# Output products of the last token block in one pass, kv beside x, and four banks for h, in a tuned attention-and-MLP kernel

## The chip, the cores and the metric

The kernel runs on one core of one Trainium2 chip. The metric is device time in microseconds (us), the median over several executions. An execution is marked slow where it is clearly longer than others of its kernel or shows a lower granted TensorE clock; all runs of this study were of the fast state, at a granted clock of 0.998 to 1.00. Verdicts are "faster", "same" or "slower" at 2%, with a 95% interval. Engines are named as in the profile: PE is TensorE, PEld its weight loads, DVE VectorE, ACT ScalarE, POOL GpSimd, SP SyncE.

## The reference, cut to what matters

```python
def _attn_ref(q, k, v):            # (8 batches, 8 heads, 576 tokens, 64)
    q_s = softmax(q, axis=-1)      # over the head's 64 elements
    k_s = softmax(k, axis=2)       # over the tokens
    kv = np.einsum('bhsd,bhse->bhde', k_s, v)
    return np.einsum('bhsd,bhde->bhse', q_s, kv)

def _moe_ref(x, w_in, w_out, beta):     # x: 4608 x 512, d_ff = 2048
    h = x @ w_in
    g = h * (1.0 / (1.0 + np.exp(-beta * h)))
    return g @ w_out
```

(The softmax lines are shortened here: the reference subtracts the maximum and divides by the sum.) So each batch needs a small product kv, a product x of q with kv, and then two large products, h and the output, which is accumulated in "acc".

## The kernel before

Tokens go through in nine chunks of 512: batches 0 to 6, then the 64 last tokens of every batch as one chunk, then batch 7. A chunk has 16 slices j of the hidden layer. For each j, PE makes h (four matmuls of 128x128 weights and 512 columns), ACT makes tanh of it, DVE makes g from tanh and h, and PE adds g's product with w_out to four acc banks, one for each block of 128 tokens ("block 0" to "block 3"). PSUM, the memory that the matmuls write, is used here as eight banks: four for acc, two called "h" and two called "att", each pair used in turn. In the code below, comments are added and cuts marked:

```python
    HB, AB = ["b1", "b2"], ["b0", "b3"]
    turns = {"h": 0, "att": 0}

    def bank(tag):
        if tag not in turns:
            return tag
        turns[tag] += 1
        return (HB if tag == "h" else AB)[(turns[tag] - 1) % 2]

    def kv_mm(b):                       # 40 matmuls in tiles of 128x64, 65 columns
        t = att_of[b] = ps.tile([P, HP, D1], F32, tag=bank("att"), bufs=1, name=f"kv{b}")
        # ... cut: loops over heads and token blocks, tile_position=(0, r * D)

    def kv_norm(b):                     # two DVE instructions that read kv's bank
        # ... cut

    def x_quad(c):                      # 8 matmuls in tiles of 64x64, 512 columns
        xr = [ps.tile([P, MAIN], F32, tag=bank(("att", "h")[kt // 2]), bufs=1, name=f"x{c}_{kt}") for kt in range(KT)]
        # ... cut: matmuls with tile_position=(r * D, a * D), then four casts to SBUF

    def mm_b(c, j, sts=None):           # acc += g * w_out, one matmul for each token block
        # ... cut

    SEQ = {
        # ... cut
        2: 'h0 p15 h1 h2a h3a b0 h4 b1 h5 b2 h6a h7 b3 h8 b4 h9 b5 h10 b6 h11 b7 h12 b8 h13 b9 h14 b10 h15 b11 b12 x0 b13 b14',
        # ... cut
    }
```

In SEQ, h is the four matmuls of one slice (with "a" in an att bank), b the four output matmuls of one slice, p the last b of the chunk before, x the product with kv for the next chunk. Kv of the next chunk is made after h9. Between the h of a chunk the other engines also get the q and k exponentials, sums and products of coming chunks ("side" work).

The softmax here doesn't subtract the row's maximum and nothing guards it: scores larger than these inputs give would overflow.

Of the kernel before, what the change touches and what calls it, by code (L numbers as in the profile page):

```python
# [9 lines left out]
BF16 = mybir.dt.bfloat16  # L10
F32 = mybir.dt.float32
# [6 lines left out]
def kernel(  # L18
# [10 lines left out]
    nc = tc.nc  # L29
# [18 lines left out]
    if LASTMAIN:  # L48
        order[B - 1], order[B] = B, B - 1
    LASTC = order[-1]  # L50

    const = ctx.enter_context(tc.tile_pool(name="const", bufs=1))
    stage = ctx.enter_context(tc.tile_pool(name="stage", bufs=1))
# [131 lines left out]
    def k_exp(b, s, n=2):  # L185
        if s == 0:
            ek_buf(b)
        m = H // n
        h = slice(s * m, (s + 1) * m)
        nc.scalar.activation(  # L190
            ek[b][:, :, h, :].rearrange("p i h d -> p h i d"),
            k_st[b][:, h, 0 : R * D].rearrange("p h (i d) -> p h i d", i=R),
            ACTF.Exp,
        )
# [9 lines left out]
    def v_buf(b):  # L204
        t = work.tile([P, HP * RW * D1], BF16, tag="va", bufs=2, name=f"va{b}")
        if b < NW:
            va[b] = t[:].rearrange("p (j i x) -> p j i x", j=HP, i=RW)
        else:
            va[b] = t[:, 0 : R * H * D1].rearrange("p (i h x) -> p i h x", i=R, h=H)
        nc.gpsimd.memset(va[b][:, :, :, D:D1], 2.0)  # L210
# [9 lines left out]
    def v_cast(b, eng):  # L220
        evac(
            eng,
            va[b][:, :, :, 0:D].rearrange("p i h d -> p h i d"),
            v_st[b][:, :, 0 : R * D].rearrange("p h (i d) -> p h i d", i=R),
        )

    def vtail_cast(b, eng):
        e = b % 2
        rr = slice(e * TAIL, (e + 1) * TAIL)
        eng.tensor_copy(vt[(b // 2) % 2][rr, e, :, 0:D], v_st[b][rr, :, R * D : R * D + D])  # L230
# [51 lines left out]
# [5 lines that stand above are left out]
# [43 lines left out]
                kvp[r, b, j : j + n, e * D : (e + 1) * D], t[r, :, 0:D], rk[r].to_broadcast((D, n, D)), ALU.mult  # L330
            )

    def kv_mm(b):
        t = att_of[b] = ps.tile([P, HP, D1], F32, tag=bank("att"), bufs=1, name=f"kv{b}")
        for j in range(HP):
            for i in range(R + 1):
                for r in range(2):
                    hd = j // 2 * 4 + 2 * r + j % 2
                    nc.tensor.matmul(  # L339
                        t[r * D : (r + 1) * D, j, :],  # L340
                        ek[b][:, i, hd, :] if i < R else ekt[(b // 2) % 2][:, ds(hd * D, D)],
                        va[b][:, i, hd, :] if i < R else vt[(b // 2) % 2][:, b % 2, hd, :],
                        start=(i == 0),
                        stop=(i == R),
                        tile_position=(0, r * D),
                    )

    def kv_norm(b):
        t = att_of.pop(b)
        rk = work.tile([P, HP, 1], F32, tag="rk", bufs=2, name=f"rk{b}")  # L350
        nc.vector.reciprocal(rk[:], t[:, :, D:D1])
        nc.vector.tensor_tensor(kvq[:, b - NW], t[:, :, 0:D], rk[:].to_broadcast((P, HP, D)), ALU.mult)

    def x_quad(c):
        xr = [ps.tile([P, MAIN], F32, tag=bank(("att", "h")[kt // 2]), bufs=1, name=f"x{c}_{kt}") for kt in range(KT)]
        for b in range(B) if c == B else (c,):
            i, e = divmod(b, 2)
            cols = ds(b * TAIL, TAIL) if c == B else slice(0, MAIN)
            if b < NW:
                for j in range(HP):  # L360
                    nc.tensor.matmul(  # L361
                        xr[j][:, cols], kvp[:, b, j, :], qsT[c][:, i, j, ds(e * TAIL, TAIL)]
                    )
                continue
            for m in range(2):
                for a in range(2):
                    for r in range(2):
                        rr = slice(r * D, (r + 1) * D)
                        qx = qsT[c][rr, :, 2 * m + a, :]
                        nc.tensor.matmul(  # L370
                            xr[2 * m + r][a * D : (a + 1) * D, cols],
                            kvq[rr, b - NW, 2 * m + a, :],
                            qx[:, i, ds(e * TAIL, TAIL)] if c == B else qx,
                            tile_position=(r * D, a * D),
                        )
        for kt in range(KT):
            evac((nc.scalar, nc.vector)[kt % 2], x_of(c)[:, kt, :], xr[kt][:])

# [29 lines left out]
        nc.scalar.activation(th[:], h_of[c, j][:], ACTF.Tanh, scale=beta_t[:, j : j + 1])  # L408

    def g_dve(c, j):  # L410
        g = g_of[c, j] = work.tile([P, MAIN], BF16, tag="g", bufs=10, name=f"g{c}_{j}")
        nc.vector.scalar_tensor_tensor(  # L412
            out=g[:], in0=th_of.pop((c, j))[:], scalar=1.0, in1=h_of[c, j][:], op0=ALU.add, op1=ALU.mult
        )
# [6 lines left out]
    def acc_tiles(c):  # L421
        if c not in acc_of:
            acc_of[c] = [
                ps.tile([P, DM], F32, tag=bank(f"acc{st}"), bufs=1, name=f"acc{c}_{st}") for st in range(R)
            ]
            if c == LASTC:
                acc_of[c].append(ps.tile([P, DM], F32, tag=bank("att"), bufs=1, name=f"acc{c}_{R}"))
                AB[:] = [AB[turns["att"] % 2]] * 2
        return acc_of[c]

    def mm_b(c, j, sts=None):
        acc = acc_tiles(c)
        sts = range(len(acc)) if sts is None else sts
        g = g_of[c, j]
        for st in sts:
            if c == LASTC and st >= R - 1:
                hw = DM // 2
                nc.tensor.matmul(  # L438
                    acc[st][:, 0:hw],
                    g[:, ds((R - 1) * P, P)],  # L440
                    w_out_b[:, j, ds((st - R + 1) * hw, hw)],
                    start=(j == 0),
                    stop=(j == NJ - 1),
                )
                continue
            nc.tensor.matmul(  # L446
                acc[st][:],
                g[:, ds(st * P, P)],
                w_out_b[:, j, :],
                start=(j == 0),  # L450
                stop=(j == NJ - 1),
            )

    o_of = {}

# [67 lines left out]
    def load_next(n):  # L523
        if order[n] < B:
            load_q(order[n])
        else:
            load_qtail()
        if n < B:
            load_kv(k_st, k, n, "k_st")
            load_kv(v_st, v, n, "v_st")  # L530

    def finish_b(c, j):
        mm_b(c, j)
        if j == NJ - 1:
            for st in range(R):
                store(c, st)
# [304 lines left out]
    tail_zero(0)  # L841
    tail_zero(1)

    def side(n, u):
        if n + 1 >= NCH:
            return
        qc = order[n + 1]
        kb = n + 1
        w = u
        if w == 2:  # L850
            q_exp(qc, 0)
            q_sum(qc, 0)
        if w == 3:
            q_exp(qc, 1)
        if w == 4:
            q_sum(qc, 1)
            if kb < B:
                k_exp(kb, 0)
                v_buf(kb)
                v_cast(kb, nc.gpsimd)  # L860
                vtail_cast(kb, nc.gpsimd)
        if w == 5:
            q_mul(qc, 0)
            if kb < B:
                ktail_exp(kb)
        if w == 6:
            if kb < B:
                k_exp(kb, 1)
        if w == 7:
            q_mul(qc, 1)  # L870
            q_xbar(qc)
        if u == 9 + (n == 1) and kb < B:
            kv_mm(kb)
            kv_norm(kb)
        if u == 9 and n + 2 < NCH:
            load_next(n + 2)

    LEAD = 4
    for u in range(LEAD):
        side(1, u)  # L880
    HOLD = 8
    SEQ = {
        1: 'h4 b2 h5 h6a b3 h7 b4 h8a h9 b5 h10 b6 h11 b7 h12 b8 h13 b9 h14 b10 h15 b11 b12 x0 b13 b14',
        2: 'h0 p15 h1 h2a h3a b0 h4 b1 h5 b2 h6a h7 b3 h8 b4 h9 b5 h10 b6 h11 b7 h12 b8 h13 b9 h14 b10 h15 b11 b12 x0 b13 b14',
        B: 'h0 p15 h1 h2a b0 h3 b1 h4 b2 h5 b3 h6 b4 h7 b5 h8 b6 h9 b7 h10 h11 h12a h13 h14 h15a',
    }

    for n in range(1, NCH):
        c = order[n]
        for w in SEQ.get(n, SEQ[2]).split():  # L890
            kind, j = w[0], int(w[1:].rstrip("a"))
            if kind == "h":
                mm_a(c, j, tag="att" if w[-1] == "a" else None)
                side(n, j)
            elif kind == "b":
                mm_b(c, j)
            elif kind == "p":
                finish_b(order[n - 1], j)
            elif kind == "x":
                x_quad(order[n + 1])  # L900
    for j in range(HOLD, NJ - 1):
        mm_b(LASTC, j, [0])
    mm_b(LASTC, HOLD, [1])
# [34 lines left out]
```

## Time and profile before

| what | value | where from |
|---|---|---|
| time | 282.59 us (282.36 to 282.81), 3 runs | times |
| PE busy | 273.9 of 280.8 us | page, busy table |
| DVE, ACT busy | 175.3, 162.0 us | same |
| one chunk, h0 to next h0 | 29.15 us | busy time by stretch |
| large matmuls in a chunk | 128, starts 0.216 us apart | PE timeline |
| kv and x in a chunk | 0.86 and 0.65 us | PE timeline |

The prediction below shows the lines for these. Two further groups tell how much room the other engines have; the columns are busy us, mean ns of one, and the idle time of the engine before them with what ended it:

```profile
L412 DVE SCALAR_TENSOR_TENSOR g<-th,h 128x512 bf16<-128x512 bf16 x144 | 97.0, 680 | 83.3 <-ACT th L408 81.4
L408 ACT ACTIVATE th<-h,beta_t 128x512 bf16<-128x512 f32 x144 | 97.9, 686 | 88.3 <-PE h L398 85.2
```

DVE waited 81.4 us for tanh, and ACT 85.2 us for h. Both follow PE. They have room, but a change in PE's order can still make PE wait for them at one place.

### The profile page before, as it was taken

How to read it: one execution, taken by the hardware profiler on the slowest of the kernel's cores; microseconds unless marked ns; L12 is line 12 of the kernel's file. 1: busy time of each engine (PE TensorE's matmuls, PEld its weight loads, DVE VectorE, ACT ScalarE, POOL GpSimd, SP SyncE). 2: the span in 40 equal slices, each digit the busy share in tenths (PEclk: the TensorE clock that was granted, in tenths of full speed). 3: DMA queues.
4: the chain of work that ended last, by engine and by line, in shares of the span. 5: the costliest groups of instructions: out<-in, count | busy, mean ns of one | idle time of the engine just before them, and what ended most of it. 6: DMA issues, size and time to landing. Idle time of an engine off the chain costs nothing.

```text
span 280.8 us, 4419 instructions
## 1 busy us (share of the span) xinstructions
PE 273.9 (98%) x1699; PEld 128.2 (46%) x1728; DVE 175.3 (62%) x284; ACT 162.0 (58%) x248; POOL 38.7 (14%) x58
## 2 busy tenths in 40 slices
PE   8999999999999999999999999999999999999995
PEld 2644454444444444444444444444444544444543
DVE  3964786993498338934794469536964596354361
ACT  3767975953495439633873478337933574454451
POOL 1554237130030003000300030002100000000000
DMA  7999999929932994099309940698153034005003
GB/s 251 391 387 392 387 388 314 295 55 289 227 149 21 273 263 158 9 269 283 154 1 218 327 153 15 141 247 250 76 123 104 0 152 75 0 0 152 0 0 149
DMA packets 55172, 50.09 MB, mean 178 GB/s; under 512 B 26600, under 2 KB 47344, under 8 KB 55152
## 3 DMA queue, kind: packets, MB, share of 16 engines
q1 hardware_dynamic: 54224, 48.91, 58.3%
q10 hardware_dynamic: 928, 0.92, 0.9%
q8 instruction: 13, 0.21, 0.3%
q14 instruction: 7, 0.06, 0.1%
HBM read 36.71 MB, written 9.44 MB: 164 GB/s over the span
## 4 chain that ended last, share of the span: by engine, by line
PE 94%; DMA 3%; issue 1%; POOL 1%; SPq 0%; ACT 0%
PE h L398 44%; PE acc L446 43%; DMA v_st<-in_v_dram 3%; PE kv L339 2%; PE x L370 1%; PE acc L438 1%; PE kv L314 1%; PE x L383 1%; POOL va L171 1%; PE tp L295 0%; SPq L129 0%; SPq L106 0%; ACT o L169 0%; PE x L361 0%; PE tb L552 0%
## 5 line engine op out<-in xcount | busy, mean ns | idle before, releaser
L412 DVE SCALAR_TENSOR_TENSOR g<-th,h 128x512 bf16<-128x512 bf16 x144 | 97.0, 680 | 83.3 <-ACT th L408 81.4
L408 ACT ACTIVATE th<-h,beta_t 128x512 bf16<-128x512 f32 x144 | 97.9, 686 | 88.3 <-PE h L398 85.2
L398 PE MATMUL h<-xT,w_in_b 128*128 128x512 bf16 x569 | 141.0, 379 | 0.3
L446 PE MATMUL acc<-w_out_b,g 128*128 128x512 bf16 x538 | 136.3, 379 | 1.9 <-issue 1.1
L398 PEld LDWEIGHTS <-w_in_b 128*128 128x128 bf16 x576 | 56.3, 98 | 66.4 <-ACT w_in_b L169 0.6
L446 PEld LDWEIGHTS <-g 128*128 128x128 bf16 x560 | 53.4, 98 | 65.0 <-issue 2.5
L171 POOL CAST va<-v_st 128x2048 bf16<-128x2048 f32 (+2 forms) x14 | 17.5, 1261 | 145.7 <-DMA v_st<-in_v_dram 145.7
L259 DVE TENSOR_REDUCE rq<-eq 128x16 f32<-128x1024 bf16 (+1 forms) x20 | 22.1, 1105 | 5.6 <-ACT eq L248 5.2
L265 DVE TENSOR_TENSOR eq<-eq,rq 128x1024 bf16<-128x1024 bf16 (+1 forms) x20 | 22.8, 1142 | 0.1
L248 ACT ACTIVATE eq<-q_st 128x1024 bf16<-128x1024 f32 (+1 forms) x18 | 16.9, 956 | 3.2 <-DMA q_st<-in_q_dram 3.2
L169 ACT CAST xT<-x 128x512 bf16<-128x512 f32 x18 | 9.9, 588 | 12.1 <-PE x L370 10.1
L171 DVE CAST xT<-x 128x512 bf16<-128x512 f32 x18 | 11.6, 686 | 6.1 <-PE x L370 5.3
L171 DVE COPY o<-acc 128x512 f32<-128x512 f32 (+1 forms) x19 | 12.1, 670 | 3.3 <-PE acc L446 3.1
L169 ACT COPY o<-acc 128x512 f32<-128x512 f32 (+1 forms) x18 | 9.6, 576 | 7.5 <-PE acc L446 4.6
L190 ACT ACTIVATE ek<-k_st 128x1024 bf16<-128x1024 f32 x12 | 12.6, 1053 | 0.0
L519 PE MATMUL warm<-xT 128*128 128x512 bf16 x30 | 9.7, 483 | 1.2 <-DVE xT L600 1.2
L171 POOL CAST w_in_b<-w_in 128x512 bf16<-128x512 f32 (+1 forms) x9 | 5.9, 660 | 5.7 <-DMA w_in<-in_moe_w_in_dram 5.6
L519 PEld LDWEIGHTS <-xT 128*128 128x128 bf16 x30 | 3.4, 118 | 6.0 <-issue 3.5
L171 POOL CAST w_out_b<-w_out 128x1024 bf16<-128x1024 f32 x5 | 5.2, 1040 | 6.3 <-DMA w_out<-in_moe_w_out_dram 6.3
L183 ACT ACTIVATE ek<-k_st 128x576 bf16<-128x576 f32 x8 | 5.0, 674 | 0.6 <-DMA k_st<-in_k_dram 0.5
L260 DVE RECIPROCAL rq<-rq 128x16 f32<-128x16 f32 (+1 forms) x20 | 4.9, 243 | 0.7
L339 PEld LDWEIGHTS <-ek 128*64 128x64 bf16 x192 | 4.1, 111 | 2.5 <-issue 2.5
(48 smaller groups left out, 83.1 us busy)
## 6 DMA issues: line engine op xcount, KB each, us to landing
out_dram<-o SPq DMA_DIRECT2D x14, 512.0 KB, 3.4
q_st<-in_q_dram SPq DMA_DIRECT2D x25, 256.0 KB, 4.1
k_st<-in_k_dram SPq DMA_DIRECT2D x6, 1024.0 KB, 7.3
v_st<-in_v_dram SPq DMA_DIRECT2D x6, 1024.0 KB, 10.0
w_in<-in_moe_w_in_dram SPq DMA_DIRECT2D x6, 512.0 KB, 9.6
v_st<-in_v_dram SPq DMA_DIRECT2D x8, 288.0 KB, 8.4
w_out<-in_moe_w_out_dram SPq DMA_DIRECT2D x4, 512.0 KB, 8.8
w_out<-in_moe_w_out_dram SPq DMA_DIRECT2D x2, 1024.0 KB, 9.6
```

Of the source, the lines that this page charges most:

```text
L169: eng.copy(dst, src)
L171: eng.tensor_copy(dst, src)
L190: nc.scalar.activation(ek[b][:, :, h, :].rearrange("p i h d -> p h i d"), k_st[b][:, h, 0 : R * D].rearrange("p h (i d) -> p h i d", i=R), ...
L248: nc.scalar.activation(eq[b][:, :, s * m : (s + 1) * m, :].rearrange("p i h d -> p h i d"), q_st[b][:, s * m : (s + 1) * m, :].rearrange(" ...
L259: nc.vector.tensor_reduce(rq[b][:, 0, :, h], eq[b][:, :, h, :], axis=AX.X, op=ALU.add)
L265: eng.tensor_tensor(eq[b][:, :, h, :], eq[b][:, :, h, :], rq[b][:, 1, :, h].unsqueeze(3).to_broadcast((P, R, m, D)), ALU.mult,)
L339: nc.tensor.matmul(t[r * D : (r + 1) * D, j, :], ek[b][:, i, hd, :] if i < R else ekt[(b // 2) % 2][:, ds(hd * D, D)], va[b][:, i, hd, :] ...
L398: nc.tensor.matmul(h[:], w_unit(j, kt), x_of(c)[:, kt, :], start=(kt == 0), stop=(kt == KT - 1),)
L408: nc.scalar.activation(th[:], h_of[c, j][:], ACTF.Tanh, scale=beta_t[:, j : j + 1])
L412: nc.vector.scalar_tensor_tensor(out=g[:], in0=th_of.pop((c, j))[:], scalar=1.0, in1=h_of[c, j][:], op0=ALU.add, op1=ALU.mult)
L446: nc.tensor.matmul(acc[st][:], g[:, ds(st * P, P)], w_out_b[:, j, :], start=(j == 0), stop=(j == NJ - 1),)
L519: nc.tensor.matmul(t[:], xT[2][:, 0, 0:P], xT[2][:, 0, :])
```

## The change

The intent: kv and x are both made of small tiles, and each stands alone between large matmuls, so PE changes its tile shape four times in a chunk (each change is called a seam below). If kv stands directly before x, there are three changes. Kv must be normalized by DVE before x can use it, so the kv that stands beside x is the one for two chunks ahead. And it needs a bank that isn't one of x's four. The change gets it by leaving block 3 out of the running output products: its 16 matmuls are made in one pass, four at the chunk's end and twelve between the next chunk's first h, and its bank is free for kv until then. With three output matmuls for each j, h come faster, so h goes round all four banks. G must live until the pass, so it gets 18 buffers in place of 10. The diff, cut to its core:

```diff
-    def kv_mm(b):
-        t = att_of[b] = ps.tile([P, HP, D1], F32, tag=bank("att"), bufs=1, name=f"kv{b}")
+    def kv_mm(b, tag):
+        t = att_of[b] = ps.tile([P, HP, D1], F32, tag=bank(tag), bufs=1, name=f"kv{b}")
...
-        g = g_of[c, j] = work.tile([P, MAIN], BF16, tag="g", bufs=10, name=f"g{c}_{j}")
+        g = g_of[c, j] = work.tile([P, MAIN], BF16, tag="g", bufs=18, name=f"g{c}_{j}")
...
+    def mm_pass(c, k):
+        if k == 0:
+            acc_of[c].append(ps.tile([P, DM], F32, tag=bank(f"acc{R - 1}"), bufs=1, name=f"acc{c}_{R - 1}"))
+        for j in range(4 * k, 4 * k + 4):
+            mm_b(c, j, [R - 1])
...
-        kb = n + 1
+        kb = n + 1 if n <= FIRST else n + 2
...
     SEQ = {
-        2: 'h0 p15 h1 h2a h3a b0 h4 b1 h5 b2 h6a h7 b3 h8 b4 h9 b5 h10 b6 h11 b7 h12 b8 h13 b9 h14 b10 h15 b11 b12 x0 b13 b14',
+        2: 'h0 q1 h1 q2 h2a q3 h3a B0 h4 B1 h5 B2 h6a h7a B3 h8 B4 h9 B5 h10a B6 h11a B7 h12 B8 h13 B9 h14a B10 h15a B11 B12 B13 k0 B14 B15 P0',
...
+            elif kind in "Pq":
+                pc = c if kind == "P" else order[n - 1]
+                mm_pass(pc, j)
+                if j == R - 1:
+                    store(pc, R - 1)
...
+            elif kind == "k":
+                kv_mm(n + 2, f"acc{R - 1}")
+                xr = x_quad(order[n + 1], ("h", "att"))
+                kv_norm(n + 2)
+                x_ev(order[n + 1], xr)
```

(Cuts are marked with "...". Left out: chunk 1 makes kv2 alone and kv3 beside x, with k and v of chunk 3 fetched and exponentiated in chunk 1; chunk 6 goes back to the order of before.) B is the three matmuls of blocks 0 to 2, P and q the quarters of the pass, k is kv with x.

## The prediction

> **What bounds the kernel now.** I read the page's busy table first, then the groups, then stretches of the span cut at each chunk's first h, and last the PE timeline around the two places in a chunk where the matmul shape changes.
>
> ```profile
> PE 273.9 (98%) x1699; PEld 128.2 (46%) x1728; DVE 175.3 (62%) x284; ACT 162.0 (58%) x248; POOL 38.7 (14%) x58
> ...
> PE 94%; DMA 3%; issue 1%; POOL 1%; SPq 0%; ACT 0%
> ...
> L398 PE MATMUL h<-xT,w_in_b 128*128 128x512 bf16 x569 | 141.0, 379 | 0.3
> L446 PE MATMUL acc<-w_out_b,g 128*128 128x512 bf16 x538 | 136.3, 379 | 1.9 <-issue 1.1
> ```
>
> The chain that ended last is 94% PE work. PE's two large groups waited 0.3 and 1.9 us in the whole span, almost none of it for another engine. But a record of 379 ns overlaps the next one, so busy time alone doesn't tell whether matmuls follow each other as closely as they can. Stretches and starts do:
>
> ```profile
> 46.83:74.69 27.86, 27.56 (x168) 12.61 (x171) 18.63 (x28) 16.89 (x25) 4.63 (x8) 1.00 0.84 226
> 74.69:103.84 29.15, 28.89 (x175) 13.24 (x177) 18.57 (x28) 17.00 (x25) 2.78 (x3) 1.00 0.65 174
> 103.84:133.00 29.16, 28.90 (x175) 13.23 (x177) 18.57 (x28) 16.88 (x25) 2.65 (x3) 1.00 0.65 180
> ```
>
> Columns: start and end in us, length, then busy us of PE, PEld, DVE, ACT and POOL, granted clock, DMA share, GB/s. The second and third rows are chunks 2 and 3, from h0 to the next h0. Each has 64 h and 64 acc matmuls, 40 of kv and 8 of x. DVE is busy 18.6 of 29.15 us and ACT 17.0.
>
> ```profile
> 87.64 1.03 PE L398 MATMUL h<-xT,w_in_b 128*128 128x512 bf16 x4
> 88.59 0.32 PE L339 MATMUL kv<-va,ek 128*64 128x65 bf16 x8
> ...
> 89.22 0.20 PE L339 MATMUL kv<-vt,ekt 128*64 128x65 bf16 x2
> 89.58 0.81 PE L446 MATMUL acc<-w_out_b,g 128*128 128x512 bf16 x3 [0.16 <-issue]
> 90.22 1.03 PE L398 MATMUL h<-xT,w_in_b 128*128 128x512 bf16 x4
> ...
> 98.86 1.03 PE L398 MATMUL h<-xT,w_in_b 128*128 128x512 bf16 x4
> 99.72 1.89 PE L446 MATMUL acc<-w_out_b,g 128*128 128x512 bf16 x7
> 101.54 0.63 PE L370 MATMUL x<-qsT,kvq 64*64 64x512 bf16 x8
> 102.10 1.90 PE L446 MATMUL acc<-w_out_b,g 128*128 128x512 bf16 x8
> 103.84 1.03 PE L398 MATMUL h<-xT,w_in_b 128*128 128x512 bf16 x4
> ```
>
> Four h start at 98.86 and the next group at 99.72: 0.86 us for four, 0.216 each. 128 x 0.216 = 27.65 us. Kv: the h before it begin at 87.64 and would end their turn at 88.50; kv begins at 88.59; the h after the four acc (one record is missing, the profile shows three) begin at 90.22, so acc began at 90.22 - 0.86 = 89.36. Kv costs 89.36 - 88.50 = 0.86 us. X: the eight acc before it begin at 99.72, their turn ends at 101.45, acc goes on at 102.10: 0.65 us. Sum: 27.65 + 0.86 + 0.65 = 29.16 us, the chunk's whole length. **So PE waits for nobody in chunks 2 and 3; it is bound by its own instruction count, and only the seams at kv and x hold time that isn't matmul streaming.** Chunk 1 is the same: its 122 large matmuls x 0.216 + 1.51 = 27.86, the first row.
>
> **What the Trainium skill says.** (1) TensorE: Matmul & The Clock Gate, Part 1, section "Wait — 56ns, not 53.3ns?": warm matmuls of 512 columns start about 215.7 ns apart. The trace agrees with 0.216, at granted clock 1.00. So no reordering makes the 128 large matmuls of a chunk shorter. (2) Perfetto Trace Analysis, Identifying the Most-Contended Engine: matmul busy share is a poor measure because matmuls are pipelined. It agrees: the mean record is 379 ns at a spacing of 216. (3) The first page again, Part 2, step 1: weight loads are pulled ahead of matmuls in flight when row groups don't conflict or the background buffer is the target. The trace agrees for the large ones (weight loads cost no spacing), but at the shape changes the loader stood idle 0.42 us "issue" and the first x load begins with the first x matmul, at 101.54; there nothing is pulled ahead. (4) PSUM — Partial Sum Buffer, "PSUM bank collisions raise a hardware error": guard PSUM by bank. Sharing a bank between kv and the last token block therefore must bring waits; no run yet shows their size.
>
> **The change, part by part.**
>
> *Matmuls.* Chunk by chunk the number and shape are unchanged: three acc per j during the chunk, and 16 for block 3 in one pass, four before the next h0 and four after each of the next chunk's h0, h1, h2. Kv of chunks 3 to 7 moves from after h9 of the chunk before to before x two chunks ahead, so chunk 1 makes kv2 and kv3 and chunk 6 none. Total change of large matmuls: 0.
>
> *Seams.* Before, four per chunk: into kv 88.59 - 88.50 = 0.09; kv's last start is about 89.24 (two records of 0.20 from 89.22), acc at 89.36, so out of kv 0.12; into x 101.54 - 101.45 = 0.09; x is two rounds of four quadrants, an estimate of 2 x 0.216 = 0.43, so out of x 102.10 - 101.97 = 0.13. Sum 0.43. After, kv and x are neighbours: in 0.09, between 0 and 0.12 from kv to x (both are small tiles, but 128x64 against 64x64, so a drain may remain), out 0.13. Saved per chunk 0.09 to 0.21; I take 0.14. Five times: **0.7 us**. That is all that the change removes from PE's path.
>
> *New waits.* I laid one chunk out by hand, 0 at h0. An h takes 0.86, B 0.65, q 0.86. From the trace: h start to tanh start 1.06, tanh to g start 0.72, g 0.69 (0.60 apart when back to back), so an h's bank is free about 2.5 us after h begins if the engines are free. With B of three, late h come every 1.51 us instead of 1.73. Two banks in turn would give 3.0 us for 2.5; four give about 6. The tightest part is h3 to h8, where q and k exponentials (1.05 each on ACT), sums (1.22 + 0.25) and products (1.21) sit between, and the store of block 3 (0.65) now falls on DVE after the first sum. DVE: sum at 6.2 to 7.6, store to 8.2, g3 ends 8.9, g4 9.5, sum to 10.9, g5 11.5, product to 12.6, g6 13.2, g7 13.8, product to 15.0, g8 15.6. PE asks: B3 (g3) at 11.4, h7 (bank of h3) at 10.6, h8 (bank of h4) at 12.1, B4 at 13.0, h9 (g5) 13.6, h10 (g6) 15.1, B6 16.0, h11 (g7) 16.6, B8 (g8) 19.0. Smallest slack 1.7 us.
>
> *End of chunk.* Let kv start at 0. Its last end is about 0.83, normalizing on DVE (0.18 + 0.42) ends near 1.5, the two x casts of DVE near 2.7, those of ACT near 2.4. X takes 0.77 to 1.33; B14 and B15 end at 2.6, so the pass may enter kv's bank 1.1 us after it is free; h0 begins at 3.5 with its third and fourth x slice wanted later still: at least 0.8 us left. The last g before x ends about 0.4 us before kv begins, and x needs that bank later. The stores of blocks 0 to 2 end by 0.5 us of the next chunk; B0 wants the banks at 6.0.
>
> *Chunk 1.* K and v of chunk 3 are fetched now and exponentiated at h11 to h13. Before, the same fetch order left the DMA nearly idle at 56 to 63 us (the 55 GB/s slice), so the 2.3 MB should land near 61 (an estimate at about 350 GB/s, after v2's 54.8); the first exponential comes near 63.6. Room of some 5 us for k, less for v, which kv3 wants at 70. ACT is 0.3 to 0.4 us late there, inside the bank slack.
>
> Sum: 282.6 - 0.7 = **281.9 us**.
>
> **Rivals.** *A: nothing saved.* The change of tile from kv to x drains as fully as kv to acc and the pass brings one short wait per chunk. For it: the seams cost the same with quite different small tiles. Against: into x at least 0.09 must go when the large matmuls between vanish. Result 282.4 to 282.8. *B: a new wait takes its place.* DVE becomes the bound around h3 to h8 or at kv's bank. For it: DVE is nearly full there, and a delay of a product by a POOL cast was 0.7 us (chunk 1's first pair of products). Against: slack of 1.7, 1.1 and 0.8 us. If 0.3 us appear in each of five chunks: 283.4. *C: chunk 1's k or v comes late*, and ACT, being in order, holds up tanh: 1 to 4 us once, 283 to 286. Against: the idle DMA slice. *D: more than the seams* is won because the pass gives PE work at chunk starts. Against: before has no gap there (29.15 is fully accounted for), so nothing can be won; below 281.2 I'd have no account.
>
> **Range and chances.** Main path 281.5 to 282.1 (65%), A some 15%, B 13%, C 5%, D 2%. With a run spread of 0.2 us: 281.2 to 282.8. Two per cent is 5.65 us; all seams of the kernel together are smaller, so faster by that is nearly excluded, and slower needs a bad case of B or C.
>
> **What would show it.** Right: chunks 2 to 5 last about 29.0 us from h0 to h0 in place of 29.15; chunk 1 gets 0.7 longer by kv3 and 1.7 shorter by eight acc matmuls that it hands on (60 before its end, 52 now), and chunk 6 takes those eight and loses kv's 0.86; kv and x stand together costing about 1.37 in place of 0.86 + 0.65; the idle times of h and acc stay under 3 us. Wrong: acc or h rows waiting on DVE, or a k_st wait of tanh's engine in chunk 1; or a chunk whose large matmuls are spaced at other than 0.216.

## The result, and the profile after

The changed kernel took 282.28 us (282.04 to 282.40, 4 runs), the kernel before 282.60 in the same rounds. The ratio is 0.9988, with an interval from 0.9971 to 1.0005. A ratio here is the mean time of one kernel's fast runs over that of the other's of the same rounds, so it is not quite the ratio of the medians. The same code in another five rounds gave 282.22 against 282.56, ratio 0.9984 (0.9971 to 0.9998).

From the page of the changed kernel, the busy table, the chain's engines and PE's two large groups:

```profile
PE 275.9 (98%) x1728; PEld 128.6 (46%) x1728; DVE 175.1 (62%) x284; ACT 162.8 (58%) x248; POOL 38.7 (14%) x58
...
PE 98%; DVE 1%; ACT 0%; issue 0%
...
L403 PE MATMUL h<-xT,w_in_b 128*128 128x512 bf16 x576 | 143.2, 379 | 0.0
L452 PE MATMUL acc<-w_out_b,g 128*128 128x512 bf16 x560 | 141.0, 379 | 0.0
```

The bound is the same. PE's busy time seems to have grown by 2.0 us and its idle time to have vanished, but neither is real: this trace has all 1728 matmul records, the one of before only 1699. A record missing at the start of a row, after small tiles, looks like a gap of 0.16 us "issue", and seven such gaps made 1.1 of the 1.9 us of idle that acc showed before. The other 15 of the 22 acc records missing there fit the rest: inside a row of matmuls, a missing record leaves 2 x 0.216 - 0.379 = 0.05 us. Starts don't have this fault. The stretches, cut at the chunk starts (columns as in the prediction):

```profile
47.20:74.08 26.88, 26.88 (x203) 12.52 (x202) 19.57 (x31) 20.03 (x30) 6.74 (x8) 1.00 1.10 273
74.08:103.13 29.05, 29.05 (x177) 13.31 (x176) 18.45 (x28) 17.11 (x25) 2.65 (x3) 1.00 0.78 198
103.13:132.18 29.05, 29.05 (x178) 13.29 (x177) 18.46 (x28) 17.23 (x25) 2.78 (x3) 1.00 0.65 172
```

Chunks 2 and 3 last 29.05 us in place of 29.15 and 29.16; chunks 4 and 5 also 29.05. Now the PE timeline at the end of chunk 2, where kv stands before x (start us, length us, group):

```profile
97.61 2.11 PE L452 MATMUL acc<-w_out_b,g 128*128 128x512 bf16 x9
99.65 0.32 PE L341 MATMUL kv<-va,ek 128*64 128x65 bf16 x8
...
100.27 0.20 PE L341 MATMUL kv<-vt,ekt 128*64 128x65 bf16 x2
100.40 0.63 PE L372 MATMUL x<-qsT,kvq 64*64 64x512 bf16 x8
100.96 2.33 PE L452 MATMUL acc<-w_out_b,g 128*128 128x512 bf16 x10
```

The nine acc from 97.61 end their turn at 97.61 + 9 x 0.216 = 99.55; kv begins at 99.65, x at 100.40, acc at 100.96. So kv costs 0.85 with its entry and x 0.56, together 1.41 where before it was 0.86 + 0.65 = 1.51. **The missing 0.10 is the entry into x; the rest is the same to 0.01 us.** From kv's last start (about 100.28, of two records from 100.27) to x are 0.12 us, as many as from kv to the large matmuls before.

A control stands in the same trace, at the end of chunk 6, where an x of full 128x128 tiles and only 64 columns follows acc:

```profile
216.17 1.89 PE L452 MATMUL acc<-w_out_b,g 128*128 128x512 bf16 x8
217.90 0.40 PE L363 MATMUL x<-qsT,kvp 128*128 128x64 bf16 x8
```

216.17 + 8 x 0.216 = 217.90, so this x begins with no delay: it is the change of tile shape that costs, not the change of product or of the number of columns. What the engine does in that 0.1 us is not shown. The weights of this x are loaded from 217.68 on, 0.22 us ahead, while the first kv weights are loaded at 99.64, together with kv's first matmul. The delay could be matmuls under way that must end first, or weights that come late; no run tells these apart.

Where the time of the whole span went, from one trace of each kernel: the part before chunk 1's first long run of h lasts 46.83 us before and 47.20 after (+0.37); chunk 1, 27.86 and 26.88 (-0.98: kv3 comes in with 0.75, eight acc matmuls of 0.216 go to chunk 6); chunks 2 to 5, four times -0.10; chunk 6 (190.27 to 220.47 after, 191.29 to 220.63 before, by the h starts), 29.34 and 30.20 (+0.86). The rest differs by 0.04. Sum: -0.2, the difference of the spans 280.8 and 280.6. So in this pair of traces the five seams gave about 0.5 us, and the start of the kernel, whose instructions the change leaves as they are, took 0.37 of it back. Whether that is chance is one question of the experiments.

The DVE timeline of chunk 2 (it begins at 74.08) shows the slack that the prediction had worked out by hand:

```profile
81.69 0.63 DVE L173 COPY o<-acc 128x512 f32<-128x512 f32 x1
...
86.51 1.28 DVE L417 SCALAR_TENSOR_TENSOR g<-th,h 128x512 bf16<-128x512 bf16 x2
...
100.52 0.18 DVE L353 RECIPROCAL rk<-kv 128x4 f32<-128x4 f32 x1 [1.30 <-PE kv L341]
100.74 0.42 DVE L354 TENSOR_TENSOR kvq<-kv,rk 128x256 bf16<-128x256 f32 x1
```

Block 3's store ends 8.2 us into the chunk, g7 (the second of the two at 86.51) at 13.7, and kv is normalized 1.5 us after kv's first matmul at 99.65; the predicted values were 8.2, 13.8 and 1.5.

### The profile page after: what moved, and what is told of

The parts are those of the page before. It is cut to its first block, busy times and chain, and to the rows that moved or that the text cites. A ratio compares the mean times of both kernels' runs of the same rounds, so it can differ in the third digit from the quotient of the medians.

```text
span 280.6 us, 4450 instructions
## 1 busy us (share of the span) xinstructions
PE 275.9 (98%) x1728; PEld 128.6 (46%) x1728; DVE 175.1 (62%) x284; ACT 162.8 (58%) x248; POOL 38.7 (14%) x58
## 4 chain that ended last, share of the span: by engine, by line
PE 98%; DVE 1%; ACT 0%; issue 0%
PE h L403 44%; PE acc L452 43%; PE warm L531 3%; PE kv L341 2%; PE x L372 1%; PE acc L444 1%; PE kv L316 1%; PE x L388 1%; PE tp L297 1%; DVE eq L267 0%; DVE qsT L173 0%; ACT o L171 0%; DVE xT L612 0%; PE x L363 0%; PE tb L564 0%
## 5 line engine op out<-in xcount | busy, mean ns | idle before, releaser
L403 PE MATMUL h<-xT,w_in_b 128*128 128x512 bf16 x576 | 143.2, 379 | 0.0
L452 PE MATMUL acc<-w_out_b,g 128*128 128x512 bf16 x560 | 141.0, 379 | 0.0
```

The lines of the kernel that those rows point to most:

```text
L403: nc.tensor.matmul(h[:], w_unit(j, kt), x_of(c)[:, kt, :], start=(kt == 0), stop=(kt == KT - 1),)
L452: nc.tensor.matmul(acc[st][:], g[:, ds(st * P, P)], w_out_b[:, j, :], start=(j == 0), stop=(j == NJ - 1),)
```

## The experiments

The theory after the result: PE is bound by its own instructions; what a change can move is the number of shape changes; each costs about 0.1 us. Rivals: the pass itself helps at a chunk's start; the gain is scatter; the larger buffers cost something that hides more gain; the four banks aren't needed. "Chunk" below is the distance from one x to the next in the trace, over chunks 2 to 5 where all are alike; each run's times stand beside the kernel before in the same rounds on the same chip.

### Repeats: the changed kernel, and the kernel before against itself

No edit in either.

> The changed kernel once more, with more rounds. Theory (one seam less in each of five chunks, 0.10 us each as the two traces show): chunks of 29.05 us and 0.5 us less than the kernel before, ratio 0.998. Rival (nothing is won, the 0.3 us of the first timing were spread): ratio 1.000. A second look is at the part before chunk 1: in the first trace it was 0.37 us longer than in that of the kernel before; if that was chance, it goes or turns here.

> The kernel before, word for word, against itself: how much do the ratio and the part before chunk 1 scatter with nothing changed. Theory (that part scatters with the first loads' landing): ratio within 0.001 of 1, chunk 1's first large run of h anywhere from 46.6 to 47.4 us, chunks of 29.15. Rival (the part before chunk 1 is firm for one program): the run of h starts within 0.1 us of 46.83.

The changed kernel again: 282.22 us (281.99 to 282.35), before 282.56, ratio 0.9984 (0.9971 to 0.9998), chunks of 29.05 us. Chunk 1's run of h begins at 47.17. The kernel before against itself: 282.67 (282.48 to 282.87), ratio 0.9996 (0.9984 to 1.0009), chunks of 29.15, run of h at 46.97. The gain is small but stands: the interval of the repeat leaves out 1. The start of the kernel isn't firm for one program, 46.83 and 46.97 in two traces of the same code.

### 18 buffers in the kernel before

```diff
-        g = g_of[c, j] = work.tile([P, MAIN], BF16, tag="g", bufs=10, name=f"g{c}_{j}")
+        g = g_of[c, j] = work.tile([P, MAIN], BF16, tag="g", bufs=18, name=f"g{c}_{j}")
```

> The kernel before with 18 buffers for g in place of 10, nothing else. Theory: the buffers only let the pass keep its g; ratio 1.000, chunks of 29.15 us, the part before chunk 1 as in the kernel before. Rival (the other addresses in SBUF cost 0.3 to 0.4 us in the part before chunk 1, which hides most of the gain of the changed kernel): ratio 1.001 and chunk 1's first large run of h starts near 47.2 us, not 46.8.

> The kernel before with 18 g buffers again, on the chip of the run above. Theory (scatter only): ratio 0.999 to 1.001. Rival (the addresses cost 0.3 us before chunk 1): ratio 1.001 again, run of h starting near 47.3.

The first run looked like the rival: 282.82 us (282.52 to 283.16), ratio 1.0009 (0.9997 to 1.0022), run of h at 47.34. The second, on the chip of the repeat of before, didn't: 282.72 (282.66 to 283.06), ratio 0.9999 (0.9987 to 1.0012), run of h at 47.01. Chunks were 29.15 in both. So the buffers cost nothing that shows, though the intervals would let 0.3 us hide in the whole time. From that run of h to the issue of the last output both runs take 231.22 to 231.23 us, as the kernel before does, so what was longer in the first run lies before chunk 1. Over all 14 traces that run of h begins between 46.67 and 47.34 us, and both ends come from kernels with 18 buffers. The differences are there early: the first kv matmul of batch 0 starts at 11.07 us in the trace of before and 11.29 in that of the changed kernel, with the same code up to there. What makes that start scatter was not settled; the first loads' landing is a guess that no run isolated.

### The pass alone

```diff
-        kb = n + 1 if n <= FIRST else n + 2
+        kb = n + 1
-        if n <= FIRST and u == 9 + (n == 1):
+        if kb < B and u == 9 + (n == 1):
             kv_mm(kb, "att")
...
             elif kind == "k":
-                kv_mm(n + 2, f"acc{R - 1}")
                 xr = x_quad(order[n + 1], ("h", "att"))
-                kv_norm(n + 2)
                 x_ev(order[n + 1], xr)
```

(The early loads of chunk 3 go as well; the loads are those of the kernel before.)

> The pass, the four h banks and the 18 g buffers stay, but kv goes back to one chunk ahead, after h9 in an att bank, and x stands alone. Theory (only the neighbourhood of kv and x pays): chunks of 29.15 us and the time of the kernel before, ratio 1.000. Rival (the pass gives PE work at a chunk's start and pays by itself): chunks of 29.05 us, ratio 0.998.

282.73 us (282.49 to 283.49), ratio 1.0010 (0.9997 to 1.0022), chunks of 29.15 to 29.16. The PE timeline has x alone again:

```profile
97.83 2.10 PE L452 MATMUL acc<-w_out_b,g 128*128 128x512 bf16 x9
99.86 0.63 PE L372 MATMUL x<-qsT,kvq 64*64 64x512 bf16 x8
```

From 97.83 + 9 x 0.216 = 99.77 to 99.86 the 0.09 us of x's entry are back. The pass, the four banks and the buffers gain nothing and cost nothing by themselves; they make room.

### One seam pair more: kv in two halves

```diff
             elif kind == "B":
+                if j == NJ - 3:
+                    kv_mm(n + 2, f"acc{R - 1}", range(HP // 2))
                 mm_b(c, j)
...
             elif kind == "k":
-                kv_mm(n + 2, f"acc{R - 1}")
+                kv_mm(n + 2, f"acc{R - 1}", range(HP // 2, HP))
```

(Cut: kv_mm takes the range as a new argument and keeps its bank between the two calls.)

> The changed kernel with kv in two halves, the first before B13's three matmuls and the second after them: one seam pair more in each of five chunks. Theory (a seam costs 0.09 us going in and 0.12 coming out, whatever the work between): chunks of 29.05 + 0.21 = 29.26 us, 1.05 us more than the changed kernel, ratio to the kernel before about 1.002. Rival (seams cost nothing of their own, kv's time goes with its count): chunks stay at 29.05.

283.21 us (283.07 to 283.60), ratio 1.0025 (1.0013 to 1.0038); chunks of 29.27. The PE timeline of the same place:

```profile
97.93 1.46 PE L454 MATMUL acc<-w_out_b,g 128*128 128x512 bf16 x6
99.32 0.32 PE L343 MATMUL kv<-va,ek 128*64 128x65 bf16 x8
...
99.63 0.20 PE L343 MATMUL kv<-vt,ekt 128*64 128x65 bf16 x2
99.76 0.82 PE L454 MATMUL acc<-w_out_b,g 128*128 128x512 bf16 x3
100.51 0.32 PE L343 MATMUL kv<-va,ek 128*64 128x65 bf16 x8
```

Three acc from 99.76 end their turn at 100.41, and the second half of kv begins at 100.51: 0.10 going in. From kv's last start (about 99.64) to acc it is 0.12. One pair more makes a chunk 29.27 - 29.05 = 0.22 us longer with the same matmuls, against 0.21 expected. **The seam has a cost of its own: it is about the same around 20 kv matmuls, around 40, and around x.**

### X before kv

```diff
-                kv_mm(n + 2, f"acc{R - 1}")
                 xr = x_quad(order[n + 1], ("h", "att"))
-                kv_norm(n + 2)
+                kv_mm(n + 2, f"acc{R - 1}")
                 x_ev(order[n + 1], xr)
+                kv_norm(n + 2)
```

> The changed kernel with x before kv, the two still side by side. Theory (each change of matmul shape drains once, about the same time in any order): seams again 0.34 us a chunk, chunks of 29.05 us, ratio to the kernel before 0.998. Rival (what counts is which small tile comes first): chunks differ from 29.05 by 0.05 to 0.1 us either way.

282.01 us (281.96 to 282.31), ratio 0.9981 (0.9967 to 0.9995), chunks of 29.05.

```profile
97.22 2.10 PE L452 MATMUL acc<-w_out_b,g 128*128 128x512 bf16 x9
99.26 0.63 PE L372 MATMUL x<-qsT,kvq 64*64 64x512 bf16 x8
99.81 0.32 PE L341 MATMUL kv<-va,ek 128*64 128x65 bf16 x8
...
100.57 2.33 PE L452 MATMUL acc<-w_out_b,g 128*128 128x512 bf16 x10
```

Entry 99.26 - 99.16 = 0.10, x 0.55, kv with its exit 0.76: together 1.41, as with kv first. So the order of the two doesn't change the sum, and x takes the same time whether kv (0.55) or acc (0.56) follows it.

### 16 buffers, with each order

```diff
-        g = g_of[c, j] = work.tile([P, MAIN], BF16, tag="g", bufs=18, name=f"g{c}_{j}")
+        g = g_of[c, j] = work.tile([P, MAIN], BF16, tag="g", bufs=16, name=f"g{c}_{j}")
```

> The changed kernel with 16 g buffers: g j of the next chunk takes the place of g j of this one, which the pass has read by then. Theory (no wait comes of it and addresses don't matter): chunks of 29.05 us, ratio to the kernel before 0.998. Rival (the buffers' addresses matter before chunk 1): a ratio that differs from the changed kernel's 0.9984 by 0.001 with the same chunks.

> X before kv and 16 g buffers. The run with x first had the lowest time so far, 282.01, though its chunks were as long as the changed kernel's. Theory (it had an earlier start by chance): ratio 0.998 within 0.0005, chunks of 29.05. Rival (x first is better by some 0.2 us outside the chunks): ratio 0.9975 or lower here too.

(The second run also has the edit of x before kv.) Both were 282.28 us (282.08 to 282.38, and 282.01 to 282.52), ratios 0.9981 (0.9968 to 0.9993) and 0.9979 (0.9965 to 0.9993), chunks of 29.05. The rival of the second was a ratio of 0.9975 or lower; it wasn't reached, though the interval includes it, and the chunks are equal; nothing shows x first to be better than kv first. 16 buffers do as well as 18. No version beats the changed kernel by more than the scatter.

### Two banks for the late h

```diff
-        2: 'h0 q1 h1 q2 h2a q3 h3a B0 h4 B1 h5 B2 h6a h7a B3 h8 B4 h9 B5 h10a B6 h11a B7 h12 B8 h13 B9 h14a B10 h15a B11 ...
+        2: 'h0 q1 h1 q2 h2a q3 h3a B0 h4 B1 h5 B2 h6a h7 B3 h8 B4 h9 B5 h10 B6 h11 B7 h12 B8 h13 B9 h14 B10 h15 B11 ...
```

(Chunk 1 likewise. The lines go on unchanged.)

> The changed kernel with the h bank order of the kernel before: from h7 on two banks in turn. Theory (the pass squeezes the late h to one every 1.51 us, and DVE is behind by the q work then): in the changed trace g7 ends at 87.79 while h9 starts at 87.68 and g8 ends near 89.5 while h10 starts at 89.19, so h9 to h10 wait 0.2 to 0.4 us in all; chunks of 29.25 to 29.45, 0.8 to 1.6 us more than the changed kernel in all. Rival (the slack is enough with two banks): chunks of 29.05.

283.62 us (283.45 to 283.99), ratio 1.0037 (1.0023 to 1.0050), chunks of 29.43, so 0.38 longer than with four banks. PE and DVE timelines in chunk 2:

```profile
87.14 0.81 PE L452 MATMUL acc<-w_out_b,g 128*128 128x512 bf16 x3
87.95 1.02 PE L403 MATMUL h<-xT,w_in_b 128*128 128x512 bf16 x4
88.81 0.81 PE L452 MATMUL acc<-w_out_b,g 128*128 128x512 bf16 x3
89.68 1.02 PE L403 MATMUL h<-xT,w_in_b 128*128 128x512 bf16 x4
```

```profile
86.61 1.28 DVE L417 SCALAR_TENSOR_TENSOR g<-th,h 128x512 bf16<-128x512 bf16 x2
87.81 1.22 DVE L267 TENSOR_TENSOR eq<-eq,rq 128x1024 bf16<-128x1024 bf16 x1
88.94 1.47 DVE L417 SCALAR_TENSOR_TENSOR g<-th,h 128x512 bf16<-128x512 bf16 x2
```

H9 should begin at 87.14 + 3 x 0.216 = 87.79 and begins at 87.95, just after g7 (the second of the two at 86.61) ends at 87.89. H10 should begin at 88.81 + 0.65 = 89.46 and begins at 89.68, after g8 (the first of the two at 88.94, of 0.69 us, so about 89.63). That is 0.16 + 0.22 = 0.38 us, the whole difference. The four banks are a needed part of the change: without them the chunk would be 0.28 us longer than before it. A reading lesson goes with this: the list of waits of this run has no entry for h on DVE at all, because the record before still "runs" for 0.16 us by its modelled end and covers most of the gap, so waits of 0.1 to 0.2 us show in starts only.

### Kv beside x without the pass

```diff
                 ps.tile([P, DM], F32, tag=bank(f"acc{st}"), bufs=1, name=f"acc{c}_{st}")
-                for st in range(R - (c in PASS))
+                for st in range(R)
...
-                kv_mm(n + 2, f"acc{R - 1}")
-                xr = x_quad(order[n + 1], ("h", "att"))
-                kv_norm(n + 2)
+                kv_mm(n + 2, "att")
+                kv_norm(n + 2)
+                xr = x_quad(order[n + 1], ("h", "att"))
```

(The order of h and b is that of the kernel before, with k in x's place. The 18 buffers stay.)

> Kv two chunks ahead and next to x as in the changed kernel, but no pass: all four acc banks are in use, so kv takes an att bank that x needs right after. Theory (the pass is the price of a free bank): the second half of x waits for kv's normalizing on DVE, some 0.6 us a chunk, against 0.1 for the seam: chunks of 29.6 to 29.8 us, 2 to 3.5 us more than the kernel before. Rival (normalizing hides behind the first half of x): chunks of 29.05 to 29.15.

285.06 us (284.81 to 285.37), ratio 1.0086 (1.0072 to 1.0100), chunks of 29.64.

```profile
102.64 0.62 PE L372 MATMUL x<-qsT,kvq 64*64 64x512 bf16 x5
103.45 0.41 PE L372 MATMUL x<-qsT,kvq 64*64 64x512 bf16 x3 [0.20 <-DVE kvq L354]
103.79 1.90 PE L452 MATMUL acc<-w_out_b,g 128*128 128x512 bf16 x8
```

The first five x begin at 102.64; the sixth is the first that needs kv's bank, and it and the two behind it begin only at 103.45, after DVE has normalized kv (the second instruction ran from 102.97 for 0.42 us, to 103.39). X takes 103.79 - 102.64 = 1.15 us in place of 0.56: 0.59 more, which is the 29.64 - 29.05 of the chunks. So the neighbourhood alone would lose five times what it gains; the bank from block 3 is what makes it pay.

### The whole pass at the chunk's end

```diff
-        2: 'h0 q1 h1 q2 h2a q3 h3a B0 h4 B1 ... k0 B14 B15 P0',
+        2: 'h0 h1 h2a h3a B0 h4 B1 ... k0 B14 B15 P0 P1 P2 P3',
```

(Chunk 1 and the start of chunk 6 likewise.)

> The changed kernel with all sixteen matmuls of the pass at the chunk's end, none between the next chunk's h0 to h3. Theory (PE is never short of work at a chunk's start, the pass only fills): by hand the tightest place has still 1 us of slack, so chunks of 29.05 us and the changed kernel's time. Rival (the spread of the pass is needed, since h0 to h7 come faster than DVE can do g and the q work): a wait for g shows at B3 to B6 and chunks are longer than 29.2.

282.27 us (282.15 to 282.29), ratio 0.9986 (0.9973 to 1.0000), chunks of 29.05. Where the pass stands makes no difference: at a chunk's start PE has enough to do, and the twelve matmuls that the change spreads there fill no gap.

## Why the prediction was right, point by point

The measured 282.28 (and 282.22) lies in the range 281.2 to 282.8 and is 0.4 and 0.3 above the 281.9. It is just above the main path's 281.5 to 282.1 too, nearer to rival A's 282.4 than to the middle. "Same" was the easy part: even 286, the longest time that any rival named, is only 1.2% off.

**The bound.** Right. Chunks 1 to 5 of both kernels are accounted for by matmul starts of 0.216 us and by seams. The pass alone and the whole pass at the end left the chunk length to the seams alone. Rival D, more than the seams, is refuted by them.

**The seams.** The step was right in kind and too large in size. The term "saved per chunk 0.09 to 0.21; I take 0.14" measured 0.10, its low end, because the passage from kv to x kept its full 0.12. The prediction was not at one with itself here: its layout of the chunk's end has x begin 0.77 after kv and end at 1.33, which with 0.09 for the entry is 1.42 and leaves only 0.09 saved; its sum used 1.37. It had left open whether two small tile kinds drain against each other, that is, whether the one must be finished before the other begins. A page that it had not looked up answers that: the Trainium skill, TensorEngine Tiling (Array Packing), Tiling Modes, "Key Properties", says that a change of tiling mode, unlike a change of tile within a mode, drains the engine. Kv is 128x64 and x 64x64, so it is a change of mode. The trace agrees on the delay, 0.12 from kv's last start to x, and not on its cause, which no run here shows. Five times 0.10 is 0.5 us in place of 0.7. The ratios of the changed kernel's three timings (0.9988, 0.9984, and 0.9981 with 16 buffers) correspond to 0.3 to 0.5 us at 282.6.

**New waits.** Right. No wait appeared in chunks 2 to 5; the values worked out by hand agree with the trace within 0.2 us. The prediction's fourth point had inferred that sharing block 3's bank must bring waits. None showed: kv was normalized at 100.74 + 0.42 = 101.16, and the pass reached the bank at 100.96 + 6 x 0.216 = 102.26. Sharing a bank with x instead, in the run without the pass, did cost 0.59. The two-bank run shows that the bank count was no formality: with two banks PE waits 0.38 us in each chunk at h9 and h10, and the whole gain is lost almost four times over. The prediction had argued the need for four banks from late h alone (3.0 us in turn against 2.5); the wait really comes from DVE being behind after the q products.

**Chunk 1.** Right in its outcome, off in one estimate. V of chunk 3 was to have landed near 61 us at about 350 GB/s, a rate for which it showed no line; in the changed kernel the slice from 56 to 63 us moved 292. In the trace, POOL waited for it until 65.66 and its second cast ended at 68.25, still 2.35 us before kv3 began at 70.60. ACT's exponential of k3 began at 63.95 without idle time before it.

**Rival A** was half right: the passage from kv to x does cost as much as from kv to acc. Its other half, a wait at the pass, didn't come, and the entry into x did go. **Rivals B and C** didn't come about. B is what the change would be with two banks.

**The range** did its work through the scatter of the start: that alone moved by 0.7 us over the traces here, more than the effect. The scatter is gone if one measures from chunk 1's run of h to the issue of the last output, here for the kernel before and the changed one:

```profile
278.05 0.37 ACTq L500 DMA_DIRECT2D out_dram<-o  x1
```

```profile
277.89 0.36 ACTq L512 DMA_DIRECT2D out_dram<-o  x1
```

278.05 - 46.83 = 231.22 us, and 277.89 - 47.20 = 230.69. All five traces with kv and x apart (the kernel before twice, 18 buffers twice, the pass alone) give 231.22 to 231.23, all six in which the two stand together at no new wait 230.69 to 230.70. So the saving is 0.53 us, and neither the buffers, the banks nor the pass move it.

## What to carry to other kernels

When matmul starts are already evenly spaced, count what interrupts the spacing: here each change of tile shape cost about 0.1 us, and putting the small-tile groups side by side saved just one such change per chunk. Such a regrouping is worth what its buffers cost: check what bank it takes and who must free it, since a bank shared with the next product cost 0.59 us a chunk and two banks too few 0.38. To measure an effect of 0.2%, use the period between repeated events in the trace, which held to 0.01 us, and not the total, whose runs of one kernel spread over 0.1 to 1.0 us.

## What the Trainium skill lacked or had wrong

- TensorEngine Tiling (Array Packing), Tiling Modes: it says that changing the mode drains TensorE but not what that costs. Here going from 128x128 into small tiles took 0.09 to 0.10 us beyond the usual spacing, and from the last start of small kv tiles to the next shape took 0.12; 128x64 to 64x64 counts as a full change; one pair more made a chunk 0.22 us longer.
- TensorE: Matmul & The Clock Gate, "Back-to-back issue gap": it gives about 131 ns for each matmul of 512 columns in a stream of weight loads and matmuls, and calls 216 too high. Here, with a new weight load for every matmul, large matmuls that waited for nothing started 0.216 us apart in every run.
- Perfetto Trace Analysis, the timeline of a TensorE instruction, says that the end of a matmul is estimated; it lacks the consequence that short waits vanish. Records of 379 ns at a spacing of 216 hid waits of 0.16 and 0.22 us from the list of waits, and missing records (29 before) made seven gaps of 0.16 us that weren't there.
- No page tells how much a kernel's start scatters: the same code reached chunk 1 at 46.83 and 46.97 us, and all kernels here at 46.67 to 47.34.
